# One load and six tiles for K, Q and V, and an issue order that expects loads later

## The chip, the cores and the metric

The kernel runs on one core of a Trainium2 chip. Its engines are TensorE (PE in the profile: matrix products, with PEld for its weight loads), VectorE (DVE), ScalarE (ACT), GpSimd (POOL) and SyncE (SP), which here only issues DMAs. Each engine takes its instructions in the order in which they stand in its program and waits on semaphores for the others. The metric is the device time of one execution in microseconds (us), the median over runs.

## The reference

Eight sequences of 576 tokens with eight heads of 64 go through causal attention with a window of 128 positions and a linear bias by distance. The result, 4,608 tokens of 512 numbers, goes through an MLP with a ratio of polynomials as activation:

```python
scores = scale * q @ k.T                       # per batch and head
mask = (rel >= 0) & (rel < 128)
scores = where(mask, scores - slope[h] * abs(rel), -1e9)
attn = softmax(scores)                         # sum + 1e-9 in the denominator
x = (attn @ v)                                 # to 4608 x 512
h = x @ w_in                                   # 512 -> 2048
g = (a0 + a1*h + a2*h**2 + a3*h**3) / (1 + |b0|*|h| + |b1|*h**2 + 1e-6)
out = g @ w_out                                # 2048 -> 512
```

The weights w_in and w_out come in 64-bit floats, which the kernel reads as pairs of 32-bit words.

## The kernel before, in words

Tokens lie in 36 blocks of 128. The MLP works on 17 tiles of them: the first and the last of three blocks, the others of two (`MLP`). Attention works on units: two heads (one of four pairs) and one or two blocks (`TILES`). The first tile has eight units: four of its first block, which use the tiles kq_first and v_first, and four of the other two blocks. Every other unit loads its keys and queries into a tile kq and its values into a tile v, four tiles of each in turn (lines 372 to 378).

A unit goes like this: TensorE makes the scores (sc, line 432); VectorE adds the bias and finds the row's extreme (line 458); ScalarE takes the exponential (line 463); VectorE takes sums and reciprocals (st, lines 471 and 472); POOL scales the probabilities (pr, line 473); TensorE transposes them (pt, line 484); ScalarE copies them out (p_all, line 488); POOL masks both copies (line 492); TensorE multiplies with the values (px, line 517); ScalarE and VectorE write x (lines 525 and 527).

The weights are cut in 16 chunks. Loads raw_w0 to raw_w31 bring them: an even number 2c is the w_in half of chunk c, the odd one 2c + 1 its w_out half (the name has the number only up to 15). Each is converted from 64 to 32 bits: POOL scales the upper words (line 578), ScalarE converts the lower (cv, line 579), VectorE joins them (lines 580 and 581, w32 or w in the trace). From load 16 on, w_in loads share one buffer and w_out loads another, so that each is issued when the one before it has been converted.

In the first tile's MLP (plain fp32) each chunk has an up-projection (h, lines 621 and 627), the activation, which ends with VectorE's g (line 657), and a down-projection for three blocks into three accumulators (acc, line 677). On the way POOL makes the gating terms (g_q, lines 645 and 647). The tiles h stand in three PSUM slots, one of which holds the third accumulator during the first tile. After that the weights are split into a high and a low part (lines 595 and 596, w_spare and w_lo, on POOL or VectorE), and all other tiles use three products of the parts.

The order of all this is set by a planner (`Plan.order`). Every operation has a due time, engines on which it may run with a cost on each, and what it depends on. The planner walks through time and gives each engine the ready operation that is due first. Due times come from some 35 numbers (A0, JL, C0, S0 and so on). The emitted program then keeps each engine's order; the chip sets the times. SP issues all DMAs; the eight semaphores for them are used in turn.

## Time and profile before

| | us |
|---|---|
| median of 3 runs (1047.11 to 1050.35) | 1047.44 |
| profiled execution | 1048.82 |
| its span, first to last instruction | 1047.1 |
| PE busy (97%) | 1019.4 |
| DVE busy (75%) | 781.3 |
| ACT busy (64%) | 671.9 |
| POOL busy (49%) | 511.5 |

Busy time is the union of an engine's instructions. A busy TensorE is not TensorE at its peak, since matmuls overlap and their ends are modelled. The granted clock is the share of TensorE's full clock (2.4 GHz) that it was given; 0.5 is 1.2 GHz. Idle time before an instruction is put down to the engine or DMA whose semaphore came last.

### The profile page before, as it was taken

What the parts mean: (1) busy time and instruction counts of PE and PEld (TensorE: products, weight loads), DVE (VectorE), ACT (ScalarE), POOL (GpSimd) and SP (SyncE); (2) the same over time, 40 slices, a digit from 0 to 9 for tenths busy, and PEclk for the clock granted to TensorE, in tenths of its full rate; (3) what the DMA queues carried; (4) which work ended last, traced back from release to release, by engine and by line L of the source; (5) the groups of instructions that cost most, each with busy time, mean ns of one, the idle gap of its engine ahead of it and who ended that gap; (6) DMA issues with size and microseconds to landing.
All of it is one profiled execution on the core that took longest, in us unless ns stands there. A gap on an engine that the chain in (4) does not pass through costs nothing.

```text
span 1047.1 us, 21020 instructions
## 1 busy us (share of the span) xinstructions
PE 1019.4 (97%) x7687; PEld 852.1 (81%) x7687; DVE 781.3 (75%) x1921; ACT 671.9 (64%) x1574; POOL 511.5 (49%) x579
## 2 busy tenths in 40 slices
PE   6799989999999999999999999999999999999998
PEld 4554458888888888888888888888888888888997
DVE  4887878877777777777777777777777777776775
ACT  5665678666666666666666666666665666666664
POOL 2754498544444444444444444444444444454442
PEclk7899999999999999999999999999999999999999
DMA  8815421111111121111110211111121112110000
GB/s 291 294 36 183 148 73 41 47 42 44 64 47 61 47 72 46 62 44 64 46 56 28 66 46 57 56 41 62 46 67 39 46 44 63 43 65 2 21 1 30
DMA packets 45271, 68.86 MB, mean 66 GB/s; under 512 B 4464, under 2 KB 29936, under 8 KB 45168
## 3 DMA queue, kind: packets, MB, share of 16 engines
q1 hardware_dynamic: 45168, 67.52, 19.6%
q8 instruction: 60, 0.98, 0.4%
q14 instruction: 43, 0.35, 0.1%
HBM read 58.07 MB, written 9.44 MB: 64 GB/s over the span
## 4 chain that ended last, share of the span: by engine, by line
PE 89%; DMA 3%; ACT 2%; DVE 2%; POOL 2%; issue 1%; SPq 0%; DVEq 0%; ACTq 0%; POOLq 0%
PE h L621 38%; PE acc L677 36%; PE px L517 7%; PE sc L432 5%; PE pt L484 3%; DMA raw_w<-in_w_in 2%; DMA raw_w<-in_w_out 1%; POOL w_lo L596 1%; ACT cv L579 1%; ACT pr L463 0%; DMA id_sb<-in_ident 0%; POOL g_q L647 0%; PE h L627 0%; DVE w L581 0%; POOL pr L473 0%
## 5 line engine op out<-in xcount | busy, mean ns | idle before, releaser
L621 PE MATMUL h<-x_hi,wi_hi 128*128 128x256 f32 (+1 forms) x1024 | 305.4, 298 | 2.5 <-ACT o L705 1.9
L621 PE MATMUL h<-x_lo,wi_hi 128*128 128x256 f32 (+1 forms) x1024 | 291.4, 285 | 0.0
L645 POOL TENSOR_SCALAR g_q<-g_u,babs 128x512 f32<-128x512 f32 (+1 forms) x152 | 115.2, 758 | 336.0 <-ACT g_u L644 328.7
L621 PE MATMUL h<-x_hi,w_lo 128*128 128x256 f32 (+1 forms) x960 | 272.8, 284 | 0.0
L621 PEld LDWEIGHTS h<-x_lo,wi_hi 128*128 128x128 f32 x1024 | 192.9, 188 | 38.9 <-issue 1.4
L621 PEld LDWEIGHTS h<-x_hi,wi_hi 128*128 128x128 f32 x1024 | 192.8, 188 | 36.6 <-issue 12.6
L677 PE MATMUL acc<-wo_hi,g_h 128*128 128x512 f32 x528 | 207.9, 394 | 0.0
L677 PE MATMUL acc<-wo_hi,g_l 128*128 128x512 f32 x528 | 200.5, 396 | 0.0
L677 PE MATMUL acc<-w_lo,g_h 128*128 128x512 f32 x495 | 194.5, 393 | 0.0
L647 POOL TENSOR_TENSOR g_q<-g_q,g_u 128x512 f32<-128x512 f32 (+1 forms) x152 | 189.3, 1245 | 9.5
L653 DVE SCALAR_TENSOR_TENSOR g_q<-g_q,h 128x512 f32<-128x512 f32 (+1 forms) x152 | 100.2, 659 | 122.6 <-ACT h L652 119.8
L621 PEld LDWEIGHTS h<-x_hi,w_lo 128*128 128x128 f32 x960 | 182.0, 190 | 0.0
L644 ACT ACTIVATE g_u<-h 128x512 f32<-128x512 f32 (+1 forms) x152 | 87.8, 577 | 111.9 <-PE h L621 110.9
L650 ACT ACTIVATE g_u<-g_q,guard 128x512 f32<-128x512 f32 (+1 forms) x152 | 106.5, 701 | 82.4 <-POOL g_q L647 79.5
L648 DVE TENSOR_TENSOR g_p<-h,g_p 128x512 f32<-128x512 f32 (+1 forms) x152 | 100.6, 662 | 69.0 <-ACT g_p L646 68.1
L473 POOL TENSOR_TENSOR pr<-pr,st 128x512 f32<-128x512 f32 (+1 forms) x76 | 76.2, 1003 | 89.5 <-DVE st L472 49.2
L463 ACT ACTIVATE pr<-pr,st 128x128 f32<-128x128 f32 x288 | 112.4, 398 | 8.5 <-DVE st L458 8.1
L646 ACT ACTIVATE g_p<-h,na 128x512 f32<-128x512 f32 (+1 forms) x152 | 114.9, 756 | 0.0
L492 POOL TENSOR_SCALAR_AFFINE_SELECT p_all<-p_all 128x512 f32<-128x512 f32 (+1 forms) x144 | 90.3, 627 | 50.3 <-ACT p_all L488 47.6
L661 ACT CAST g_h<-h 128x512 fp32r<-128x512 f32 (+1 forms) x136 | 78.7, 579 | 53.2 <-DVE h L660 53.0
L649 DVE SCALAR_TENSOR_TENSOR g_p<-g_p,na,h 128x512 f32<-128x512 f32 (+1 forms) x152 | 108.7, 715 | 2.7
L654 DVE SCALAR_TENSOR_TENSOR h<-g_p,na,h 128x512 f32<-128x512 f32 (+1 forms) x152 | 109.5, 721 | 0.0
(69 smaller groups left out, 1601.0 us busy)
## 6 DMA issues: line engine op xcount, KB each, us to landing
kq<-in_kqv SPq DMA_DIRECT2D x68, 320.0 KB, 3.3
v<-in_kqv SPq DMA_DIRECT2D x68, 192.0 KB, 2.6
out<-o SPq DMA_DIRECT2D x33, 256.0 KB, 2.0
raw_w<-in_w_in SPq DMA_DIRECT2D x16, 512.0 KB, 4.5
raw_w<-in_w_out SPq DMA_DIRECT2D x16, 512.0 KB, 5.8
bias_t<-in_bias SPq DMA_DIRECT2D x44, 64.0 KB, 2.3
kq<-in_kqv SPq DMA_DIRECT2D x4, 192.0 KB, 2.4
out<-o SPq DMA_DIRECT2D x6, 128.0 KB, 1.8
```

The costliest lines, as they stand in the source:

```text
L463: nc.scalar.activation(ap(pr)[:, y, :], ap(pr)[:, y, :], AF.Exp, bias=ap(st)[:, y : y + 1], scale=-1.0, accum_out=ap(st)[:, 4 + y : 5 + y])
L492: plan.op(A + D2 + 0.6 - 0.1 * k, cost, lambda e, k=k, sign=sign: nc.gpsimd.affine_select(out=side(k), in_=side(0), pattern=[[0, 2], [0, m ...
L621: nc.tensor.matmul(h(n), w[:, k, :], x[:, k, :], start=(k == 0 and m == 0), stop=(k == NKC - 1 and m == len(seq) - 1))
L645: plan.op(E, {"g": tsc}, lambda e: nc.gpsimd.tensor_scalar(v(g_q), v(g_u), ap(babs)[:, 1:2], ap(babs)[:, 0:1], ALU.mult, ALU.add), reads=[ ...
L646: plan.op(E, {"a": act(W, 1, 2) - 20}, lambda e: nc.scalar.activation(v(g_p), v(h_s), AF.Identity, bias=ap(na)[:, 2:3], scale=ap(na)[:, 3: ...
L647: plan.op(E, {"g": ttc}, lambda e: nc.gpsimd.tensor_tensor(v(g_q), v(g_q), v(g_u), ALU.mult), reads=[(g_q, 0), (g_u, 0)], writes=[(g_q, 0)])
L648: plan.op(E, {"v": dve(W)}, lambda e: nc.vector.tensor_tensor(v(g_p), v(h_s), v(g_p), ALU.mult), reads=[(h_s, 0), (g_p, 0)], writes=[(g_p, ...
L649: plan.op(E, {"v": dve(W, 1)}, lambda e: stt(v(g_p), v(g_p), ap(na)[:, 1:2], v(h_s), ALU.add, ALU.mult), reads=[(h_s, 0), (g_p, 0)], write ...
L650: plan.op(E, {"a": act(W, 0, 1)}, lambda e: nc.scalar.activation(v(g_u), v(g_q), AF.Ln, bias=guard, scale=1.0), reads=[(g_q, 0)], writes=[ ...
L653: plan.op(E, {"v": dve(W)}, lambda e: stt(v(g_q), v(g_q), GUARD, v(h_s), ALU.add, ALU.mult), reads=[(g_q, 0), (h_s, 0)], writes=[(g_q, 0)])
L654: plan.op(E, {"v": dve(W, 1)}, lambda e: stt(v(h_s), v(g_p), ap(na)[:, 0:1], v(h_s), ALU.add, ALU.mult), reads=[(g_p, 0), (h_s, 0)], write ...
L677: nc.tensor.matmul(ap(accs[t][i]), x[:, sl], w, start=(c == 0 and part == 0 and m == 0), stop=(c == NFC - 1 and (part == 1 or t == 0) and ...
```

## The change

For every unit but those of the first block, K, Q and V come in one load of 512 KB into one tile of 1,024 columns, and there are six such tiles. For the first block the keys and queries come in two loads in place of four, and the values in one. In the planner a load's user is taken to start 1,500 ns after the load's end (30 before), and SP is taken to be busy while eight loads are under way. Most of the numbers for due times have new values.

```diff
+LANES = 8
...
+        ("s", "p"): 1500, ("s", "v"): 1500, ("s", "a"): 1500, ("s", "g"): 1500,
...
                     if e == "s":
-                        free_at[e] = t + 475
                         dma_free = max(dma_free, t + 475 + 650) + cost
                         o.end = dma_free + 1000
+                        landed.append(o.end)
+                        free_at[e] = max(t + 475, landed[-LANES] if len(landed) >= LANES else 0.0)
...
-    sb4 = ctx.enter_context(tc.tile_pool(name="sb4", bufs=4))
+    sbk = ctx.enter_context(tc.tile_pool(name="sbk", bufs=6))
...
-    C0, DC, CO, DO, WL = 2.025, 6.35, 24.27, 5.33, 4.229
-    S0, DS, SL, AW, BL = 120.399, 2.316, 3.017, 27.807, 7.326
+    C0, DC, CO, DO, WL = -2.492, 6.391, 23.755, 5.295, 4.229
+    S0, DS, SL, AW, BL = 113.646, 2.291, 2.644, 27.807, 7.466
...
-            plan.op(u0 - JL, {"s": 364}, lambda e: eng[e].dma_start(ap(first_kq)[:, p], src[:, P : 3 * P]), writes=[(first_kq, p)])
-            plan.op(u0 - JL + VL, {"s": 182}, lambda e: eng[e].dma_start(ap(first_v)[:, p], src[:, 4 * P :]), writes=[(first_v, p)])
+            if p == 0:
+                firsts = kqv[o : o + NPAIR * P * W].rearrange("(p q w) -> q p w", p=NPAIR, q=P)
+                for g in ((0, 1), (1, NPAIR)):
+                    plan.op(u0 - JL, {"s": 364 * (g[1] - g[0])}, lambda e, g=g: eng[e].dma_start(ap(first_kq)[:, g[0] : g[1]], firsts[:, g[0] : g[1], P : 3 * P]), writes=[(first_kq, y) for y in range(*g)])
+                plan.op(u0 - JL + VL, {"s": 728}, lambda e: eng[e].dma_start(ap(first_v), firsts[:, :, 4 * P :]), writes=[(first_v, y) for y in range(NPAIR)])
...
-        kq = slot(sb4, [P, KMAX + QMAX], F32, "kq")
-        v = slot(sb4, [P, KMAX], F32, "v")
-        after = 1000 * (u0 - AW) if t else 0.0
-        plan.op(u0 - JL, {"s": 2002 * (W - ks) / 1408}, lambda e: eng[e].dma_start(ap(kq)[:, : W - ks], src[:, : W - ks]), writes=[(kq, 0)], after=after)
-        plan.op(u0 - JL + VL, {"s": 2002 * ks / 1408}, lambda e: eng[e].dma_start(ap(v)[:, :ks], src[:, W - ks :]), writes=[(v, 0)], after=after)
+        kqv_sb = slot(sbk, [P, WMAX], F32, "kqv")
+        plan.op(u0 - JL, {"s": 2002 * W / 1408}, lambda e: eng[e].dma_start(ap(kqv_sb)[:, :W], src), writes=[(kqv_sb, 0)], after=1000 * (u0 - AW) if t else 0.0)
```

The order of the instructions moves on all engines. Three places are shown; in a row stand the line, the instruction, and the tiles with the numbers that tell buffers apart, written tile first. Lines of the new kernel have numbers higher by three here. A DMA's shape is in elements: four bytes each, two for the bias.

The first place is the start of the program on SP and on POOL. SP before:

```order
L368 DMA kq_first_84<-in_kqv 128x256 x3
L314 DMA bias_first_91<-in_bias 128x1024
L368 DMA kq_first_84<-in_kqv 128x256
L369 DMA v_first_96<-in_kqv 128x128
L377 DMA kq_99<-in_kqv 128x640
L369 DMA v_first_96<-in_kqv 128x128
L311 DMA id_sb_115<-in_ident 128x256
L369 DMA v_first_96<-in_kqv 128x128
L377 DMA kq_125<-in_kqv 128x640
L369 DMA v_first_96<-in_kqv 128x128
L378 DMA v_137<-in_kqv 128x384
L573 DMA raw_w0_143<-in_w_in 128x4x256
```

and now:

```order
L317 DMA bias_first_84<-in_bias 128x1024
L374 DMA kq_first_87<-in_kqv 128x256
L374 DMA kq_first_87<-in_kqv 128x3x256
L314 DMA id_sb_92<-in_ident 128x256
L576 DMA raw_w0_95<-in_w_in 128x4x256
L375 DMA v_first_98<-in_kqv 128x4x128
L381 DMA kqv_101<-in_kqv 128x1024
```

POOL before, from its first work on (pr are probabilities, units 1 to 5 in this order):

```order
L473 TENSOR_TENSOR pr_120<-pr_120,st_121 128x256
L473 TENSOR_TENSOR pr_128<-pr_128,st_129 128x256
L578 TENSOR_SCALAR raw_w0_143<-raw_w0_143 128x512
L473 TENSOR_TENSOR pr_170<-pr_170,st_171 128x256
L473 TENSOR_TENSOR pr_205<-pr_205,st_206 128x256
L578 TENSOR_SCALAR raw_w2_201<-raw_w2_201 128x512
L578 TENSOR_SCALAR raw_w4_213<-raw_w4_213 128x512
L473 TENSOR_TENSOR pr_266<-pr_266,st_267 128x512
```

and now:

```order
L581 TENSOR_SCALAR raw_w0_95<-raw_w0_95 128x512
L476 TENSOR_TENSOR pr_125<-pr_125,st_126 128x256
L476 TENSOR_TENSOR pr_144<-pr_144,st_145 128x256
L581 TENSOR_SCALAR raw_w2_110<-raw_w2_110 128x512
L476 TENSOR_TENSOR pr_188<-pr_188,st_189 128x256
L476 TENSOR_TENSOR pr_214<-pr_214,st_215 128x256
L581 TENSOR_SCALAR raw_w4_154<-raw_w4_154 128x512
L581 TENSOR_SCALAR raw_w6_161<-raw_w6_161 128x512
L476 TENSOR_TENSOR pr_258<-pr_258,st_259 128x512
```

The first weight load moves from the fourteenth place on SP to the fifth; on POOL the scaling of each early weight load moves ahead by about two instructions.

The second place is POOL in the first tile's MLP, at the gating (g_q, two instructions a chunk) of chunks 6 and 7. Before, with the loads 20 (raw_w_838), 22 (raw_w_892) and 19 (raw_w_898):

```order
L645 TENSOR_SCALAR g_q_868<-g_u_855,babs_229 128x384
L578 TENSOR_SCALAR raw_w_838<-raw_w_838 128x512
L647 TENSOR_TENSOR g_q_868<-g_q_868,g_u_855 128x384
L578 TENSOR_SCALAR raw_w_892<-raw_w_892 128x512
L578 TENSOR_SCALAR raw_w_898<-raw_w_898 128x512
L645 TENSOR_SCALAR g_q_943<-g_u_931,babs_229 128x384
L647 TENSOR_TENSOR g_q_943<-g_q_943,g_u_931 128x384
```

and now, with the loads 20 (raw_w_816), 19 (raw_w_839) and 22 (raw_w_873):

```order
L581 TENSOR_SCALAR raw_w_816<-raw_w_816 128x512
L648 TENSOR_SCALAR g_q_858<-g_u_848,babs_169 128x384
L650 TENSOR_TENSOR g_q_858<-g_q_858,g_u_848 128x384
L581 TENSOR_SCALAR raw_w_839<-raw_w_839 128x512
L648 TENSOR_SCALAR g_q_892<-g_u_884,babs_169 128x384
L650 TENSOR_TENSOR g_q_892<-g_q_892,g_u_884 128x384
L581 TENSOR_SCALAR raw_w_873<-raw_w_873 128x512
```

Load 22 moves from ahead of the gating of chunk 7 to behind it. In the same way loads 24, 28 and 30 stand one or two chunks later against the gating.

The third place is POOL at the hand-over to the second tile, from the second gating instruction of the first tile's last chunk or shortly before it to the gating of the second tile's first pair of chunks. Before:

```order
L596 TENSOR_TENSOR w_spare_1298<-w32_0_249,wi_hi_1140 128x512
L645 TENSOR_SCALAR g_q_1326<-g_u_1296,babs_229 128x384
L596 TENSOR_TENSOR w_lo1_1331<-w32_1_363,wi_hi_1140 128x512
L647 TENSOR_TENSOR g_q_1326<-g_q_1326,g_u_1296 128x384
L596 TENSOR_TENSOR w_lo2_1354<-w32_2_332,wi_hi_1140 128x512
L596 TENSOR_TENSOR w_lo2_1354<-w32_2_332,wo_hi_1162 128x512
L596 TENSOR_TENSOR w_lo3_1382<-w32_3_447,wi_hi_1140 128x512
L596 TENSOR_TENSOR w_lo4_1401<-w32_4_530,wi_hi_1140 128x512
L645 TENSOR_SCALAR g_q_1415<-g_u_1405,babs_229 128x512
L473 TENSOR_TENSOR pr_1359<-pr_1359,st_1360 128x512
L647 TENSOR_TENSOR g_q_1415<-g_q_1415,g_u_1405 128x512
```

and now:

```order
L648 TENSOR_SCALAR g_q_1318<-g_u_1312,babs_169 128x384
L599 TENSOR_TENSOR w_spare_1321<-w32_0_164,wo_hi_1046 128x512
L650 TENSOR_TENSOR g_q_1318<-g_q_1318,g_u_1312 128x384
L476 TENSOR_TENSOR pr_1287<-pr_1287,st_1288 128x512
L599 TENSOR_TENSOR w_lo2_1364<-w32_2_321,wo_hi_1046 128x512
L599 TENSOR_TENSOR w_lo3_1383<-w32_3_341,wi_hi_1039 128x512
L495 AFFINE_SELECT p_all_1376<-p_all_1376 128x4x128
L648 TENSOR_SCALAR g_q_1396<-g_u_1386,babs_169 128x512
L495 AFFINE_SELECT p_all_1376<-p_all_1376 128x4x128
L650 TENSOR_TENSOR g_q_1396<-g_q_1396,g_u_1386 128x512
```

Three splittings leave POOL between the two gatings and the probabilities move ahead of the rest; on VectorE five splittings stand before the last g of the first tile, where three stood. On TensorE, the third pair of the second tile's up-projections, which waited for ScalarE's eviction of the third accumulator, stands behind four down-projections of the second tile, and its slot is one that VectorE frees.

## Rows read from the trace of the kernel before

**Rows 1.** Busy time by stretch. Columns: stretch in us from the span's start and its length, then busy us (and instructions) of PE, PEld, DVE, ACT and POOL, the granted clock, the busy share of the DMA engines, and GB/s.

```profile
0.00:10.00 10.00, 6.93 (x42) 2.94 (x43) 1.73 (x17) 3.30 (x10) 1.43 (x6) 0.95 0.73 201
10.00:20.00 10.00, 7.45 (x78) 4.54 (x77) 4.80 (x26) 5.78 (x24) 2.49 (x4) 0.54 0.95 323
20.00:30.00 10.00, 6.18 (x70) 5.30 (x74) 7.38 (x29) 5.86 (x19) 6.54 (x10) 0.83 0.93 326
...
40.00:43.00 3.00, 2.43 (x15) 1.72 (x16) 2.93 (x5) 1.83 (x3) 2.16 (x3) 0.50 0.93 247
43.00:47.00 4.00, 4.00 (x13) 3.21 (x12) 3.90 (x7) 2.85 (x5) 2.50 (x4) 0.56 1.01 371
...
80.00:100.00 20.00, 18.99 (x84) 9.57 (x82) 16.21 (x39) 12.09 (x28) 9.14 (x12) 1.00 0.42 143
...
155.00:160.00 5.00, 4.92 (x48) 4.25 (x48) 4.92 (x7) 2.71 (x6) 4.82 (x6) 0.66 0.14 52
...
170.00:1000.00 830.00, 830.00 (x6631) 725.96 (x6631) 620.86 (x1524) 538.63 (x1256) 398.23 (x440) 1.00 0.15 49
```

**Rows 2.** Waits of TensorE, longest in total first: engine, tile and line, what it waited for, us in total, times, longest. The first three are of 0 to 43 us, the fourth of 57 to 140 us, the last four of 140 to 170 us.

```profile
PE pt L484 <- POOL pr L473: 7.9, 5, 2.5
PE px L517 <- POOL p_all L492: 4.2, 3, 2.7
PE pt L484 <- DMA id_sb<-in_ident: 2.2, 1, 2.2
...
PE h L621 <- DVE g L657: 4.3, 7, 1.2
...
PE h L621 <- ACT o L705: 1.9, 1, 1.9
PE pt L484 <- POOL pr L473: 1.1, 1, 1.1
PE h L621 <- DVE g L657: 0.4, 1, 0.4
PE h L621 <- DVE g_l L662: 0.3, 1, 0.3
```

**Rows 3.** POOL in order of time, from the start: start in us, duration in us, line, operation, tiles, shapes, and in brackets the idle time before it and what ended it.

```profile
13.59 0.65 POOL L578 TENSOR_SCALAR raw_w<-raw_w 128x512 f32<-128x512 f32 x1 [3.88 <-DMA raw_w<-in_w_in]
...
21.30 1.03 POOL L473 TENSOR_TENSOR pr<-pr,st 128x512 f32<-128x512 f32 x1
23.38 0.65 POOL L578 TENSOR_SCALAR raw_w<-raw_w 128x512 f32<-128x512 f32 x1 [1.06 <-DMA raw_w<-in_w_in]
25.51 0.65 POOL L578 TENSOR_SCALAR raw_w<-raw_w 128x512 f32<-128x512 f32 x1 [1.47 <-DMA raw_w<-in_w_out]
...
39.87 0.64 POOL L492 TENSOR_SCALAR_AFFINE_SELECT p_all<-p_all 128x512 f32<-128x512 f32 x1
```

**Rows 4.** DMA issues by line: tiles, engine, count, KB each, median us from issue to landing.

```profile
kq<-in_kqv SPq DMA_DIRECT2D x68, 320.0 KB, 3.3
v<-in_kqv SPq DMA_DIRECT2D x68, 192.0 KB, 2.6
...
raw_w<-in_w_in SPq DMA_DIRECT2D x16, 512.0 KB, 4.5
raw_w<-in_w_out SPq DMA_DIRECT2D x16, 512.0 KB, 5.8
```

**Rows 5.** TensorE in order of time: the first up-projection of the first tile that needs all of its x.

```profile
43.39 3.42 PE L627 MATMUL h<-x_hi,w 128*128 128x256 f32 x8
```

**Rows 6.** VectorE in order of time, 104 to 107 us.

```profile
104.55 0.69 DVE L580 SCALAR_TENSOR_TENSOR cv<-raw_w,cv 128x512 int32<-128x512 int32 x1 [1.97 <-ACT cv L579]
...
106.94 0.55 DVE L657 SCALAR_TENSOR_TENSOR g<-g_q,h 128x384 f32<-128x384 f32 x1
```

**Rows 7.** TensorE in order of time, the same moment.

```profile
107.55 0.91 PE L621 MATMUL h<-x_hi,w 128*128 128x384 f32 x2 [1.20 <-DVE g L657]
```

**Rows 8.** Groups of instructions by line and shape: tiles, shapes, count, busy us, mean ns of one, idle us of the engine before them and what ended most of it. The first two are VectorE's in 57 to 147 us, the third is POOL's in 57 to 170 us.

```profile
L580 DVE SCALAR_TENSOR_TENSOR cv<-raw_w,cv 128x512 int32<-128x512 int32 x19 | 12.9, 694 | 7.0 <-ACT cv L579 3.3 <-POOL raw_w L578 2.9 <-POOL g_q L647 0.7
...
L596 DVE TENSOR_TENSOR w_lo<-w,wo_hi 128x512 fp32r<-128x512 f32 x3 | 3.0, 992 | 0.2 <-POOL w_lo L596 0.2
...
L578 POOL TENSOR_SCALAR raw_w<-raw_w 128x512 f32<-128x512 f32 x16 | 10.6, 661 | 21.9 <-DMA raw_w<-in_w_in 11.7 <-DMA raw_w<-in_w_out 9.5 <-DVE st L458 0.6
```

**Rows 9.** POOL in order of time at the gating of chunks 6 and 7.

```profile
80.72 1.01 POOL L647 TENSOR_TENSOR g_q<-g_q,g_u 128x384 f32<-128x384 f32 x1
87.17 0.66 POOL L578 TENSOR_SCALAR raw_w<-raw_w 128x512 f32<-128x512 f32 x1 [5.45 <-DMA raw_w<-in_w_in]
...
89.10 0.67 POOL L645 TENSOR_SCALAR g_q<-g_u,babs 128x384 f32<-128x384 f32 x1
```

**Rows 10.** POOL in order of time at the hand-over.

```profile
144.62 3.65 POOL L596 TENSOR_TENSOR w_lo<-w,wi_hi 128x512 fp32r<-128x512 f32 x2
148.25 1.30 POOL L645 TENSOR_SCALAR g_q<-g_u,babs 128x512 f32<-128x512 f32 x1
149.52 1.57 POOL L473 TENSOR_TENSOR pr<-pr,st 128x512 f32<-128x512 f32 x1
151.05 1.74 POOL L647 TENSOR_TENSOR g_q<-g_q,g_u 128x512 f32<-128x512 f32 x1
```

**Rows 11.** The w_in loads of line 573 issued from 60 to 120 us: time from issue to landing.

```profile
DMA to landing us min/median/max: 3.7/3.9/4.2
```

More of the change, by code (lines that the diff above doesn't have):

```diff
@@ L112, in order @@
         rings, free_at = {}, {**dict.fromkeys("pavg", 0.0), "s": 650.0}
-        dma_free, busy = 0.0, {}
+        dma_free, busy, landed = 0.0, {}, []
         for o in self.ops:
@@ L260, in banded_attention_ratio_mlp @@
     ps3 = ctx.enter_context(tc.tile_pool(name="ps3", bufs=3, space=PSUM))
-    count = {id(const): 1, id(ps1): 1, id(sb2): 2, id(sb3): 3, id(sb4): 4, id(ps3): 3}
+    count = {id(const): 1, id(ps1): 1, id(sb2): 2, id(sb3): 3, id(sbk): 6, id(ps3): 3}
     eng = {"p": nc.tensor, "a": nc.scalar, "v": nc.vector, "g": nc.gpsimd, "s": nc.sync}
@@ L265, in banded_attention_ratio_mlp @@
     SESSION = 290
-    A0, DA, T0, L0, L1 = -4.886, 1.542, 22.263, 90.555, 24.911
-    AOFF, D2, D3, JL, VL = -0.627, 1.814, 7.045, 8.441, 4.671
+    A0, DA, T0, L0, L1 = -0.833, 1.536, 22.263, 90.555, 24.812
+    AOFF, D2, D3, JL, VL = -0.627, 1.941, 7.045, 7.707, 4.001
     SP, SV, SA, SG = 0.204, 0.103, 0.021, 0.16
-    LL = 6.867
-    ML, ZA, ME, OE = 23.116, 0.956, -1.043, 9.542
-    C0, DC, CO, DO, WL = 2.025, 6.35, 24.27, 5.33, 4.229
-    S0, DS, SL, AW, BL = 120.399, 2.316, 3.017, 27.807, 7.326
+    LL = 13.858
+    ML, ZA, ME, OE = 23.116, 0.956, -1.043, 9.531
+    C0, DC, CO, DO, WL = -2.492, 6.391, 23.755, 5.295, 4.229
+    S0, DS, SL, AW, BL = 113.646, 2.291, 2.644, 27.807, 7.466
     plan = Plan({"p": 1000 * SP, "v": 1000 * SV, "a": 1000 * SA, "g": 1000 * SG})
@@ L373, in job @@
             return kt, qt, vt, [(first_kq, p)], [(first_v, p)]
-        kq = slot(sb4, [P, KMAX + QMAX], F32, "kq")
-        v = slot(sb4, [P, KMAX], F32, "v")
-        after = 1000 * (u0 - AW) if t else 0.0
-        plan.op(u0 - JL, {"s": 2002 * (W - ks) / 1408}, lambda e: eng[e].dma_start(ap(kq)[:, : W - ks], src[:, : W - ks]), writes=[(kq, 0)], after=after)
-        plan.op(u0 - JL + VL, {"s": 2002 * ks / 1408}, lambda e: eng[e].dma_start(ap(v)[:, :ks], src[:, W - ks :]), writes=[(v, 0)], after=after)
-        kt = lambda c0, c1: ap(kq)[:, c0:c1]
-        qt = lambda i: ap(kq)[:, ks + i * P : ks + (i + 1) * P]
-        vt = lambda b: ap(v)[:, b * P : (b + 1) * P]
-        return kt, qt, vt, [(kq, 0)], [(v, 0)]
+        kqv_sb = slot(sbk, [P, WMAX], F32, "kqv")
+        plan.op(u0 - JL, {"s": 2002 * W / 1408}, lambda e: eng[e].dma_start(ap(kqv_sb)[:, :W], src), writes=[(kqv_sb, 0)], after=1000 * (u0 - AW) if t else 0.0)
+        kt = lambda c0, c1: ap(kqv_sb)[:, c0:c1]
+        qt = lambda i: ap(kqv_sb)[:, ks + i * P : ks + (i + 1) * P]
+        vt = lambda b: ap(kqv_sb)[:, W - ks + b * P : W - ks + (b + 1) * P]
+        return kt, qt, vt, [(kqv_sb, 0)], [(kqv_sb, 0)]
     xs = {}
```

## The prediction

> **What bounds the kernel now.** I read the table of busy time by stretch first. From 170 to 1000 us TensorE is busy 830.00 of 830.00 us at a granted clock of 1.00 [rows 1]; the reader should see that nothing can be won there by waiting less, since no wait of TensorE is left. What the change can move lies before 170 us. I then read TensorE's waits in the stretches before that. They fall into three stages [rows 2]. In the start (0 to 43 us: attention of the first three blocks, in which only TensorE's waits of 7.9 us for POOL's scaling of the probabilities, 4.2 us for its masks and 2.2 us for the identity count) the engines wait for data. In the MLP of the first tile (57 to 140 us) TensorE waits 4.3 us in all, seven times, each time for VectorE's last step g. In the hand-over to the second tile (140 to 170 us) it waits 1.9, 1.1, 0.4 and 0.3 us. The third view is POOL's timeline: in the start POOL stands in front of weight loads, 13.59, 23.38 and 25.51 us being the ends of such waits [rows 3]; since it works in order, the scaling of the probabilities (pr) stands behind them.
>
> The profiled execution took 1048.82 us (span 1047.1 us and 1.7 us around it); the median of the three timed runs is 1047.44 us. I sum changes in us against the profiled execution and take the sum off the median.
>
> **Steady state, 170 us to the end: 0.** TensorE's instructions are the same in number and shape; only their order differs here and there. Every load of K, Q and V that used to be two is now one, and SP issues 77 fewer DMAs. No TensorE wait in this stretch names a load, so fewer or earlier ones hide nothing that is now seen: what covers the loads is TensorE's own work, and six tiles in place of four only widen the cover. If the cover went, a unit's scores would wait for a 512 KB load; the nearest rows are 3.3 us for the 320 KB part and 4.5 to 5.8 us for the 512 KB weights from issue to landing, once [rows 4]. I keep 0, with 0.5 us either way.
>
> **Step 1, the start: +1.7 us.** The order moves the first weight load from the fourteenth place on SP's queue to the fifth, and POOL's rows move with it: its first instruction is now the scaling of weight load 0, ahead of the first probabilities; and before the probabilities of the fifth unit it now scales loads 4 and 6, where before it scaled loads 2 and 4. Count the KB on the queue, each load by its size (the large ones in [rows 4]; the small ones are 64 to 256 KB by their shapes in the order). Up to and with weight load 0 there were 2,496 KB, now 1,408; up to load 6 there were 5,571 KB, now 6,083; up to the last load that POOL scales before the last mask of the first tile, 10,563 (load 7) and now 11,779 (load 9). Load 0 was scaled at 13.59 us; by bytes alone it now lands at 1,408 / 2,496 x 13.59 = 7.7 us. From 20 to 30 us the queue moved 326 GB/s, 318 KB a us [rows 1]. From 7.7 us at that rate, load 6 lands at 7.7 + 4,675 / 318 = 22.4 us, and by the bytes of before (5,571 KB at 23.38 us, 6,403 KB at 25.51 us [rows 3]) at 24.7 us. Add 0.65 us for its scaling: the fifth unit's probabilities start between 23.1 and 25.3 us, where they started at 21.30 us [rows 3]: +1.8 to +4.0 us. From there to the end of the last mask POOL has four scalings of probabilities at 1.04, eight masks at 0.64 and nine weight scalings at 0.66 us, 15.2 us; before it had one weight scaling less, 14.6 us, and took from 21.30 to 40.51 us for it, so 4.6 us were waits. With no wait it would now end at 23.1 + 15.2 = 38.3 us, 2.2 us sooner. With load 9 at 22.4 + 5,696 / 318 = 40.3 us, and its scaling and two masks behind it (1.9 us), it ends at 42.2 us, 1.7 us later. The bounds are thus -2.2 and +4.0 us; I take +1.7, the value of the row of 20 to 30 us, in which the same loads were under way. The first up-projection that needs all of x (43.39 us, eight matmuls in 3.42 us [rows 5]) moves with it. It ran at the lower level of TensorE's clock: granted 0.50 and 0.56 in 40 to 47 us, 1.2 GHz for most of it, after a stretch in which TensorE waited [rows 1, 2]. Its start stays as full of waits, so I leave that cost (4 us at 0.44 lost, 1.8 us) as it is; both ends are inside the bounds above.
>
> Before 10 us the queue moved 201 GB/s, and from 10 to 20 us 323 GB/s [rows 1]; four loads of 64 KB (v_first) and five of 128 KB are among the first thirteen. The Trainium skill (DMA: Bandwidth & Descriptors, Rules for kernel authors) says to merge many small transfers into one large one. By the rows nothing says whether size or the cold start makes the first 10 us slow, so the sum above takes the rate from later; by the rule the start would gain, which is the second rival.
>
> **Step 2, the MLP of the first tile: -3.8 us.** The path is seen once in full: VectorE waits 1.97 us for a converted weight load before 104.55 us, g ends at 107.49 us, and TensorE, which waited 1.20 us for it, starts at 107.55 us [rows 6, 7]. In this stretch VectorE waits 7.0 us before such conversions and POOL 21.2 us for loads (11.7 and 9.5 us) [rows 8]. The clearest wait of POOL is 5.45 us before 87.17 us, with the gating (g_q) of the next chunk queued behind the load [rows 9]. The new order puts that load's scaling behind the gating pair of chunk 7 instead of ahead of it, which is 0.67 + 1.01 us of work in front of it, and does the like for the w_in loads of chunks 12, 14 and 15. So when a load is late, what waits for it is the conversion of a later chunk, not the g that TensorE is about to read. VectorE's own work between two g's (0.55 to 0.7 us each, conversions 0.69) does not change in sum. I keep 0.5 us of the 4.3 us: the w_in load of chunk 13 is issued when a conversion is done that stands 1.2 us ahead of a g, VectorE wants it two conversions (1.4 us) after that g, and such a load takes 3.9 us to land [rows 11]. Bounds: -4.3 us (all of it) and +1.2 us (one more stall as long as the longest).
>
> **Step 3, the hand-over: -1.0 us.** Two stalls go. The third pair of the second tile took the PSUM slot of the third accumulator, whose eviction stood on ScalarE behind a logarithm that waited for POOL (1.9 us); now it takes a slot that VectorE frees, and four down-projections of the second tile stand before it. The transposes waited 1.1 us for probabilities behind six weight splittings and a gating on POOL [rows 2, 10]; now one splitting stands before them. That is -3.0 us. What is late next is the last g of the first tile: VectorE has five splittings before it where it had three, 0.99 us each [rows 8], +2.0 us, and the second pair waits for that slot. Bounds: -3.7 us (all four waits) and +3.0 us (five splittings delay and none of the stalls goes). The lower clock after these waits, 0.66 in 155 to 160 us [rows 1], costs 5 x 0.34 = 1.7 us and lies inside the bounds.
>
> **Sum.** 1.7 - 3.8 - 1.0 = -3.1 us: 1045.7 us for the profiled execution, 1044.3 us for the median.
>
> **Rivals.**
> 1. The stalls only move. VectorE is busy 16 of 20 us in the first MLP and has little room, so a delay of 1.7 us at the start could keep it behind TensorE all along. Then step 2 gives 1.7 us and steps 1 and 3 cancel it: 1047.4 us. For it: g of one chunk is followed by TensorE's use within 0.06 us [rows 6, 7]. Against: in the new order most g's stand several VectorE instructions earlier against TensorE's use.
> 2. The start gains as well: larger and fewer loads fill the queue from the first us, so that POOL never waits after the fifth unit and step 1 is its lower bound, -2.2 us. Sum -7.0 us: 1040.4 us. For it: 323 GB/s as soon as the queue is full. Against: 201 GB/s before.
> 3. Slower: POOL's wait for load 6 in front of the fifth unit's probabilities, at the upper bound of +4.0 us, and ScalarE's conversion of load 1 in front of that unit's copy of the transposes carry through the start, while step 2 gives only 0.8 us and step 3 nothing: +3.2 us, 1050.6 us. It decides if load 6 is scaled after about 25 us. For it: POOL did wait for each of these loads. Against: after 10 us the queue has no gap that six tiles would not close.
> That the change does not do what it says is no rival: the order of SP shows one load per unit.
>
> **How the numbers follow.** Forecast 0.42, rival 1 0.21, rival 2 0.24, rival 3 0.13. A difference of 0.3%, 3.1 us, is about what a measurement of this kernel can tell from no change. The forecast stands on that line, so half of it (0.21) counts as faster and half as the same: faster 0.45, same 0.42, slower 0.13. The range reaches from rival 2 to short of rival 3: 1040.0 to 1049.5 us.
>
> **What would show it.** Step 1: POOL's scaling of load 6 at 22 to 25 us, and the up-projection of eight matmuls at 42 to 47 us. Step 2: TensorE's waits for g in the first MLP under 1 us in sum, POOL's waits for loads well under 21 us. Step 3: no wait of TensorE for the eviction of an accumulator, a new one of 1 to 3 us for the last g. Wrong would be any TensorE wait after 170 us, or a start that ends before 41 or after 47 us.

## The result and the profile after

The new kernel took 1058.21 us (median of 4 runs, 1056.88 to 1059.37) where the kernel before took 1047.28 in the same session: the ratio is 1.0091, 95% interval 1.0078 to 1.0104, so it is slower by 0.9%. The profiled execution, the fastest of the four, took 1056.88 us, its span is 1055.2 us, and it is the one that the rows below are from; the other three had spans of 1056.3 to 1057.6 us at a mean granted clock of 0.983 to 0.985, where this one had 0.989.

Busy time by stretch, of the new kernel, columns as in [rows 1], with three stretches more:

```profile
0.00:10.00 10.00, 5.20 (x33) 2.28 (x33) 2.10 (x16) 3.78 (x10) 1.42 (x6) 1.00 0.75 240
10.00:20.00 10.00, 8.21 (x86) 5.08 (x86) 5.76 (x29) 5.97 (x25) 3.10 (x5) 0.52 1.04 392
20.00:30.00 10.00, 5.38 (x48) 3.96 (x50) 6.94 (x23) 5.11 (x16) 6.95 (x11) 0.84 1.05 395
40.00:43.00 3.00, 2.64 (x16) 1.73 (x18) 1.66 (x13) 2.75 (x11) 2.36 (x5) 0.50 0.63 183
43.00:47.00 4.00, 4.00 (x24) 3.13 (x21) 3.75 (x7) 2.89 (x6) 2.09 (x3) 0.80 0.86 275
50.00:60.00 10.00, 9.10 (x52) 5.64 (x51) 7.10 (x22) 4.83 (x16) 3.79 (x6) 0.83 0.05 15
60.00:80.00 20.00, 18.74 (x88) 10.17 (x87) 18.34 (x43) 14.22 (x33) 11.60 (x15) 1.00 0.23 75
...
170.00:1000.00 830.00, 827.88 (x6614) 721.05 (x6615) 622.14 (x1521) 533.42 (x1245) 396.12 (x437) 1.00 0.15 48
```

The same for the kernel before in the stretches that [rows 1] doesn't have:

```profile
50.00:60.00 10.00, 9.66 (x59) 5.46 (x59) 8.68 (x26) 7.64 (x21) 5.53 (x8) 1.00 0.11 40
60.00:80.00 20.00, 20.00 (x91) 10.86 (x90) 16.10 (x39) 11.84 (x29) 10.45 (x14) 1.00 0.24 72
```

From 170 us on TensorE lacks 2.12 us of 830, and its last wait of the hand-over ends at 175.4 us. So here too nearly all that matters comes before 190 us. The queue moved more per us than before in all of the first 30 us (240, 392 and 395 GB/s against 201, 323 and 326), yet from 50 to 60 us TensorE is behind: 9.10 us busy at a clock of 0.83.

TensorE's waits in the new kernel: the first line is of 57 to 140 us, the others of 140 to 190 us (columns as in [rows 2]):

```profile
PE h L624 <- DVE g L660: 4.2, 4, 1.9
...
PE acc L680 <- ACT g_h L664: 2.9, 2, 2.5
PE h L624 <- DVE g L660: 2.2, 1, 2.2
PE pt L487 <- POOL pr L476: 1.6, 1, 1.6
PE h L624 <- DVE g_l L665: 1.2, 1, 1.2
```

In the first MLP the wait for g is what it was, 4.2 us for 4.3. At the hand-over four waits of 3.7 us in sum have become waits of 7.9 us. Those for g_h and for pr stand at places where there was none; those for the last g and for g_l were 0.4 and 0.3 us before.

To see where time is lost when the order differs, I counted TensorE's work: each of its instructions at its length at full clock (0.84 ns a column in the first tile's MLP, the mean from 200 to 1000 us for the others), added up in the order of the trace. Time less that sum is what was lost by then, by waits and by the clock alike. The kernel before has lost 31.9 us at 60 us, 38.4 at 140, 44.4 at 190. Against it, the new kernel:

| lost more than before, us, by | 60 us | 140 us | 190 us | 980 us |
|---|---|---|---|---|
| new kernel | +3.5 | +3.1 | +7.7 | +8.6 |

That is +3.5 in the start, -0.4 in the first MLP, +4.6 at the hand-over and 0.9 later; the spans differ by 8.1 us. The count itself is good to about 1 us. For the start a single execution is less sure than that: three of the runs below have the new kernel's order up to 60 us, and counted in the same way they had lost 4.4, 5.2 and 5.6 us more than before by then. So the figures for the start are good to about 2 us.

### The profile page after: what moved, and what is told of

It is laid out like the page before. It is cut to its first block, busy times and chain, and to the rows that moved or that the text cites. A ratio compares the mean times of both kernels' runs of the same rounds, so it can differ in the third digit from the quotient of the medians.

```text
span 1055.2 us, 20925 instructions
## 1 busy us (share of the span) xinstructions
PE 1021.3 (97%) x7687; PEld 850.9 (81%) x7687; DVE 788.0 (75%) x1925; ACT 671.4 (64%) x1574; POOL 509.1 (48%) x575
## 4 chain that ended last, share of the span: by engine, by line
PE 88%; DVE 3%; DMA 3%; POOL 2%; ACT 2%; issue 1%; SPq 0%; ACTq 0%; POOLq 0%; DVEq 0%
PE h L624 38%; PE acc L680 36%; PE px L520 6%; PE sc L435 5%; PE pt L487 3%; POOL w_lo L599 1%; DMA raw_w<-in_w_out 1%; DMA kqv<-in_kqv 1%; DVE cv L583 1%; DVE w_lo L599 1%; ACT pr L466 0%; DMA kq_first<-in_kqv 0%; ACT cv L582 0%; DVE w L584 0%; DMA raw_w<-in_w_in 0%
```

## The experiments

**Which part of the change? Each alone, in the kernel before.**

The loads alone (the edit of lines 365 to 385 with six tiles; rules and numbers as before):

> The kernel before with only the loads changed: one load of 512 KB a unit, six tiles, the merged first loads; planner and numbers as before. Theory N (the new numbers cost the time, since they put VectorE's conversions and splittings in front of what TensorE waits for): within 2 us of before, 1045 to 1049 us. Theory L (the loads cost it: what they move on the queue is late): 1053 us or more. Theory R (the planner's two rules cost it): as N here.

The planner's rules alone:

> The kernel before with only the planner's two rules changed (users of a load start 1,500 ns after it, SP is busy while eight loads are under way). Theory R: 1053 us or more. Theories N and L: within 2 us of before, 1045 to 1049 us.

The numbers alone:

> The kernel before with only the numbers for due times changed; loads and planner as before. Theory N: as slow as the new kernel, 1055 to 1060 us, most of it lost before 60 us and from 150 to 185 us. Theories L and R: 1045 to 1049 us.

Measured: 1056.80, 1053.32 and 1059.72 us, beside 1048.22 for the kernel before (ratios 1.0080, 1.0039 and 1.0106, each interval within 0.003 of it). Each theory's own run came out in its range, and the other two theories, which held that part to be free (1045 to 1049 us), were wrong about it. So no one part is the cause: each alone costs 5 to 12 us, and all three together cost 11, less than the parts' sum of 25. What they have in common is that each gives another order.

So I tried the smallest cause of another order, one number of the kernel before:

```diff
-    C0, DC, CO, DO, WL = 2.025, 6.35, 24.27, 5.33, 4.229
+    C0, DC, CO, DO, WL = 2.025, 6.35, 24.47, 5.33, 4.229
```

> The kernel before, in which a single number is changed: the due times of the w_out loads come 0.2 us later (CO 24.27 to 24.47). Loads, tiles and rules are those of before. Theory T: 4 to 9 us slower, 1051 to 1056 us, lost between 40 and 190 us. Theories L and R (a part of the change costs the time): no change, 1046 to 1049 us.

Measured: 1055.99 us beside 1048.56 (1.0064, 1.0047 to 1.0080), as Theory T said: the medians are 7.4 us apart, with the loads, tiles and rules of before. Its waits of TensorE from 140 to 190 us:

```profile
PE pt L484 <- POOL pr L473: 3.9, 2, 2.8
PE h L621 <- DVE g L657: 2.6, 2, 1.6
PE px L517 <- POOL p_all L492: 1.0, 1, 1.0
PE h L621 <- DVE g_l L662: 0.8, 1, 0.8
```

8.3 us, for 3.7 before: the same kind of waits as in the new kernel, from a shift of the due times of 16 loads and their conversions by 0.2 us.

**Can the places be mended one by one?** The next runs keep the new kernel and move a few instructions behind or ahead of others, after the planner has set the order. First the three numbers of the splittings as before:

```diff
-    S0, DS, SL, AW, BL = 113.646, 2.291, 2.644, 27.807, 7.466
+    S0, DS, SL, AW, BL = 120.399, 2.316, 3.017, 27.807, 7.466
```

> The new kernel with the three numbers S0, DS and SL of before, which set when the weights are split at the hand-over; the order up to 130 us stays. If these three cause what is lost from 150 to 185 us (4.3 us more than before), the time falls by 3 to 5 us, to 1053 to 1055 us, and the waits of 2.5 us for g_h, 1.6 us for pr and 1.2 us for g_l go. If the hand-over is slow because VectorE comes into it late, it falls by less than 1 us and waits of the same sum stand there under other names.

Measured: 1056.51 us (1.0064, 1.0044 to 1.0085), 1.7 us under the new kernel (in another session) and short of the 3 to 5 us expected. The waits for the last g, for pr and for g_l are gone; in their place stand, from 140 to 190 us,

```profile
PE acc L681 <- ACT g_h L665: 3.8, 1, 3.8
PE px L521 <- POOL p_all L496: 1.4, 1, 1.4
```

5.2 us for 7.9. After the wait of 3.8 us the clock fell, as this stretch of the same run shows:

```profile
160.00:170.00 10.00, 6.56 (x29) 5.98 (x30) 8.83 (x14) 6.86 (x13) 8.81 (x7) 0.66 0.39 132
```

2.2 us of full speed went there (6.56 busy x 0.34), most of the 2.7 us that the waits gave back. Then the conversion of load 11 behind the first chunks:

```diff
+    ahead(op["a", 11], op["a", 16])
+    ahead(op["cv", 11], op["cv", 16])
+    ahead(op["w", 11], op["cv", 16])
```

> The new kernel, in which the conversion of weight load 11 (one instruction on ScalarE, two on VectorE, 1.4 us) stands behind the first two chunks' activation, as before, and not ahead of the first. Theory Q (TensorE's time goes where VectorE or POOL have other work queued in front of the activation): VectorE's first g_p comes 1.3 us earlier, TensorE's waits of 1.1 and 0.9 us for conversions at 50 us fall by about 1.3 us in sum, and the time by 1 to 3 us, to 1055 to 1057 us. Rival (the start is set by the landing of the loads and the clock): no change, 1057 to 1059 us.

Measured: 1057.21 us (1.0083, 1.0068 to 1.0098), in the rival's range and just outside Theory Q's. At 60 us the loss was 2.1 us smaller than in the new kernel, at 80 us about the same again. (Against the three runs with the new kernel's start it was 3.1 to 4.3 us smaller at 60 us and 0.9 to 2.3 at 80.) TensorE in this run, two moments (start, duration, idle time before):

```profile
50.54 0.94 PE L436 MATMUL sc<-kqv 64*64 64x128 f32 x24 [1.17 <-DVE w L585]
...
63.42 0.91 PE L625 MATMUL h<-x_hi,w 128*128 128x384 f32 x2 [2.77 <-DVE g L661]
```

VectorE just before the second moment:

```profile
60.90 0.69 DVE L584 SCALAR_TENSOR_TENSOR cv<-raw_w,cv 128x512 int32<-128x512 int32 x1
61.62 0.69 DVE L585 SCALAR_TENSOR_TENSOR w<-raw_w,cv 128x512 int32<-128x512 int32 x1
62.22 0.69 DVE L584 SCALAR_TENSOR_TENSOR cv<-raw_w,cv 128x512 int32<-128x512 int32 x1
62.82 0.55 DVE L661 SCALAR_TENSOR_TENSOR g<-g_q,h 128x384 f32<-128x384 f32 x1
```

Three steps of conversions now stand right in front of the second chunk's g where the new kernel had one, and the wait there grew from 1.26 to 2.77 us. The gain was real, and most of it was given back by 80 us. That VectorE has hardly any room there (18.34 of 20 us in 60 to 80) may be why, but it is not shown: the best kernel below has VectorE busy for 17.53 us of the same 20, and there TensorE is busy for all 20.

At the hand-over, splittings behind what TensorE waits for (the edit names nine, of which 14 to 16 keep their place on their engine, so that six move):

```diff
+    op["lo", 6].engine = "v"
+    behind(op["lo", 7], op["g", 0, 15])
+    behind(op["lo", 6], op["g", 0, 15])
+    behind(op["lo", 13], op["g", 1, 0])
+    for k in (14, 15, 16):
+        behind(op["lo", k], op["lo", k - 1])
+    behind(op["lo", 20], op["pr", 14])
+    behind(op["lo", 22], op["g", 1, 2])
+    behind(op["lo", 25], op["gl", 1, 2])
```

> The new kernel, in which at the hand-over eight splittings stand behind an activation step or the probabilities instead of ahead of them (one of them goes from POOL to VectorE); the number of splittings is the same. Theory Q: the waits of 2.2 us for the last g, 2.5 us for g_h, 1.6 us for pr and 1.2 us for g_l fall from 7.6 to under 4 us in sum and the time by 3 to 5 us, to 1053 to 1055 us. Rival (VectorE and POOL have too much work between 145 and 175 us in any order): the sum of the waits stays over 6 us and the time within 1 us of the new kernel.

Measured: 1058.87 us (1.0099, 1.0084 to 1.0115), no gain. TensorE's waits from 140 to 190 us, the three largest:

```profile
PE acc L681 <- ACT g_h L665: 2.9, 2, 1.9
PE h L625 <- DVE g L661: 1.5, 1, 1.5
PE h L625 <- DVE g_l L666: 1.3, 2, 0.7
...
```

7.3 us in all; the big ones are smaller and others have come to them. That is the rival's outcome, though its reason (too much work in any order) will not stand.

In the first MLP, and all three edits together:

> The new kernel, in which at three places of the first tile's MLP a conversion or the next chunk's g_p steps stand behind g instead of ahead of it, and ScalarE's logarithm and exponential of chunk 8 ahead of the next chunk's absolute value. Theory Q: the three waits for g (1.3, 1.9 and 0.9 us) fall to under 1.5 us in sum and the time by 2 to 3 us, to 1055 to 1056 us. Rival (g is late because the weights are): the waits and the time stay.

> All three edits together. Theory Q: the gains add to 6 to 10 us, 1048 to 1052 us, about the kernel before. If the time that one edit frees is lost at the next stage, 1054 us or more.

Measured: 1060.78 and 1058.56 us, both above Theory Q's ranges. These two say little: the edit put the g_p steps of chunk 9 behind the exponential that overwrites what they read, so that chunk's activation is not the reference's, and g_p waits for that exponential, a wait that I had not meant to add.

Is it the count of splittings on VectorE? In the new kernel VectorE has 17 of the 32 and POOL 15, before it was 13 and 19.

```diff
+    for k in (8, 14, 18, 20):
+        op["lo", k].engine = "v"
```

> The kernel before, in which four of the 32 splittings go from POOL to VectorE, 17 in place of 13, as in the new kernel and in each of the slower ones. Theory V (the hand-over is slow because VectorE has four splittings more, 0.7 to 1.8 us each): the waits of TensorE from 140 to 190 us grow by 2 to 5 us and the time to 1049 to 1052 us. Rival (VectorE has room there, 6.94 us busy of 10 in 150 to 160 us): within 1 us of before.

Measured: 1047.50 us (0.9989, 0.9979 to 0.9999). Theory V falls; the count costs nothing where the order leaves room.

**What does a fitted order make of the same parts?** The due-time numbers were searched anew, with the planner alone, until the end by its own clock was earliest; nothing else was changed. First the merged loads with the old rules:

> The merged loads and the six tiles with the planner's rules of before and due-time numbers that were searched for anew, until the planner's own clock was shortest. Theory T (neither loads nor rules cost time; each change gives an order that nobody has fitted, and an order that is not fitted loses 5 to 12 us before 190 us): 1047 us or less, 10 us under the same loads with the old numbers (1056.8 us). Theory L (the loads cost it): 1053 us or more, since the loads are the same as there.

The new kernel's loads and both rules:

> The new kernel with loads, tiles and the two rules, and numbers searched for anew in the same way. Theory T: 1047 us or less. Theory M (the rules make the planner expect loads 3 us and more later than they land, 38.15 us for weight load 14 that landed at 36.6 us and 40.1 for load 3 that had landed at 27 us, so an order that fits the planner's clock doesn't fit the chip): slower than the retuned loads without the rules by 3 us or more, 1048 to 1056 us.

(The 40.1 us given there for load 3 is the planner's time for its use, not for its landing.) Measured: 1043.13 us (0.9941, 0.9926 to 0.9956) and 1054.09 us (1.0046, 1.0031 to 1.0061). The first has the loads, tiles and rules of the first experiment (1056.80 us) and differs from it in numbers alone: 13.7 us lie between them (ratios to before of 0.9941 and 1.0080), and in 140 to 190 us TensorE has not one wait. So the loads don't cost the time. The second came out as theory M said. So each rule by itself, the old loads as a control, and second sets of numbers:

> The merged loads and six tiles, of the two rules only the one by which SP is busy while eight loads are under way, numbers searched anew. If the 1,500 ns before a load's users is what makes the order unfit: 1042 to 1047 us. If this rule is: 1050 us or more. If only both together do: 1042 to 1047 us here and in the next run.

> The same with the other rule only, a load's users start 1,500 ns after it. If these 1,500 ns make the order unfit: 1050 us or more. If the rule on eight loads does: 1042 to 1047 us.

> Loads, tiles and rules of before, numbers searched anew in the same way and for as long as for the merged loads. Theory T (the loads are neutral, an order's fit is all): within 2.5 us of the merged loads searched anew (1043.1 us), 1041 to 1046 us. If the loads and the six tiles are worth 5 us by themselves: 1047 us or more, no better than before.

> The new kernel's loads, tiles and both rules with a second set of numbers, from another search. Theory M (both rules together make the order unfit): 1050 us or more again. If the first set was a bad draw: 1042 to 1047 us, as with each rule alone.

> Loads, tiles and rules of before with a second set of numbers, from another search. If the merged loads are worth several us in a fitted order (the start of the first set lost 4 us more by 60 us than the three fitted orders with merged loads): 1046 us or more again. If the first set was a bad draw: 1041 to 1045 us.

> The merged loads with the rules of before and numbers chosen to bear loads and engines a few per cent off the planner's own figures. If fit to the chip is what counts: as fast as the first set (1043.1 us) or up to 2 us faster, 1040 to 1044 us. If the first set was luck: 1046 us or more.

| loads, rules | numbers | us | ratio to before, 95% | lost by 60 / 140 / 190 us, against before |
|---|---|---|---|---|
| merged, old rules | searched | 1043.13 | 0.9926 to 0.9956 | -0.8 / -3.6 / -9.0 |
| merged, old rules | chosen to bear a few per cent | 1045.74 | 0.9955 to 0.9978 | +0.4 / -2.3 / -5.7 |
| merged, rule of eight | searched | 1043.24 | 0.9939 to 0.9973 | -1.9 / -4.3 / -6.1 |
| merged, rule of 1,500 ns | searched | 1045.12 | 0.9954 to 0.9978 | -1.5 / -5.0 / -8.2 |
| merged, both (new kernel) | first set | 1054.09 | 1.0031 to 1.0061 | +2.1 / -1.2 / +0.6 |
| merged, both (new kernel) | second set | 1042.87 | 0.9925 to 0.9956 | -4.5 / -6.8 / -8.7 |
| old, old | first set | 1050.03 | 1.0002 to 1.0022 | +1.4 / -0.1 / -1.3 |
| old, old | second set | 1044.32 | 0.9931 to 0.9975 | -1.0 / -2.8 / -4.3 |

Neither rule alone makes the order unfit (1043.24 and 1045.12 us). The first set for the old loads missed Theory T's 1041 to 1046 us. The numbers chosen to bear a few per cent gave 1045.74 us, between the two ranges stated for them, so that run decides nothing. Theory M falls with the second set: the same loads, tiles and rules as the new kernel, with other numbers, take 1042.87 us where the kernel before took 1049.20 on the same chip. This version beats both kernels, the new one by 1.5% (1.0091 to 0.9941, in different sessions). What the merged loads are worth by themselves stays open: the second set for the old ones gave 1044.32 us, and the 1.5 us between the best of each are less than two sets of one kind differ by (2.6 to 11 us). Theory T is what remains, and its strict form is wrong too: an end that the planner puts early is no promise, since two of the seven sets that were searched for the earliest end gave 1050 us and more. In the first set for both rules the loss comes after 190 us (+0.6 there, +5.3 at 980 us). From there to 980 us TensorE waits 0.5 us in all and has the clock at 1.00, so neither explains it, and its cause stays open.

The second set is the best kernel here. Its numbers:

```diff
-    A0, DA, T0, L0, L1 = -0.833, 1.536, 22.263, 90.555, 24.812
-    AOFF, D2, D3, JL, VL = -0.627, 1.941, 7.045, 7.707, 4.001
-    SP, SV, SA, SG = 0.204, 0.103, 0.021, 0.16
-    LL = 13.858
-    ML, ZA, ME, OE = 23.116, 0.956, -1.043, 9.531
-    C0, DC, CO, DO, WL = -2.492, 6.391, 23.755, 5.295, 4.229
-    S0, DS, SL, AW, BL = 113.646, 2.291, 2.644, 27.807, 7.466
+    A0, DA, T0, L0, L1 = 1.3196, 1.16563, 22.263, 92.8172, 24.7258
+    AOFF, D2, D3, JL, VL = 0.154072, 2.50672, 8.18304, 13.328, 8.38041
+    SP, SV, SA, SG = 0.118028, 0.0899765, -0.0379476, 0.127445
+    LL = 6.96256
+    ML, ZA, ME, OE = 27.9823, 0.924374, -3.75721, 4.54333
+    C0, DC, CO, DO, WL = 4.56286, 6.51872, 26.6176, 4.97545, 5.18672
+    S0, DS, SL, AW, BL = 122.161, 2.26931, 7.42405, 25.906, 8.5593
```

Its stretches and its first up-projection of eight matmuls:

```profile
40.00:43.00 3.00, 3.00 (x13) 2.12 (x12) 2.93 (x6) 2.12 (x4) 1.20 (x2) 1.00 0.91 288
43.00:47.00 4.00, 4.00 (x32) 2.32 (x32) 3.72 (x7) 2.39 (x5) 2.98 (x5) 1.00 0.86 300
50.00:60.00 10.00, 10.00 (x28) 5.05 (x27) 9.71 (x29) 7.62 (x20) 6.37 (x9) 1.00 0.01 2
...
39.41 1.89 PE L630 MATMUL h<-x_hi,w 128*128 128x256 f32 x8
```

Its waits of TensorE, the largest of 57 to 140 us, and the two largest of 140 to 190 us:

```profile
PE h L624 <- DVE g L660: 2.1, 2, 1.2
...
PE acc L680 <- ACT g_h L664: 1.4, 1, 1.4
PE pt L487 <- POOL pr L476: 1.3, 2, 0.7
...
```

In all they are 2.3 us in the first MLP for 4.2 in the new kernel, and 3.2 us at the hand-over for 7.9. Too much work in any order is not the reason: the run of 1045.12 us (rule of 1,500 ns) has 17 splittings on VectorE and 15 on POOL, as the new kernel has, and by 190 us it had lost 8.2 us less than the kernel before. (The best kernel has 13 and 19.) From 40 to 47 us and from 50 to 60 us it has the clock at 1.00, where the new kernel had 0.50, 0.80 and 0.83.

## Why the prediction was wrong

It said 1044.3 us, by -3.1 us on the profiled execution; that execution came out at +8.1 us. What failed is the summing of single waits: each step took one wait away or put one in, and left out what the new order puts in front of TensorE's next instructions, on VectorE in step 1, on ScalarE in step 2 and behind the last g in step 3. By its steps:

**Steady state, 0.** About right: 0.9 us lost between 190 and 980 us, a little over the 0.5 us either way. The waits of 1.6, 0.4 and 1.2 us after 170 us, named as what would show it wrong, belong to the hand-over, which lasts longer than I had drawn it.

**Step 1, +1.7 us for the start; lost 3.5 us by 60 us.** POOL's last mask of the first tile ended at 42.2 us, as the sum said, and the up-projection of eight matmuls came at the time forecast. Both came by another way, and the loss went on after them:

```profile
21.59 0.65 POOL L581 TENSOR_SCALAR raw_w<-raw_w 128x512 f32<-128x512 f32 x1 [1.95 <-DMA raw_w<-in_w_in]
...
37.45 1.04 POOL L476 TENSOR_TENSOR pr<-pr,st 128x512 f32<-128x512 f32 x1 [3.26 <-DVE st L475]
...
40.28 0.64 POOL L581 TENSOR_SCALAR raw_w<-raw_w 128x512 f32<-128x512 f32 x1
40.88 1.34 POOL L495 TENSOR_SCALAR_AFFINE_SELECT p_all<-p_all 128x512 f32<-128x512 f32 x2
...
44.86 1.89 PE L630 MATMUL h<-x_hi,w 128*128 128x256 f32 x8
```

Load 6 was scaled at 21.59 us, earlier than my 22 to 25, since from 10 to 20 us the queue moved 392 GB/s, which is 383 KB a us, and not the 318 that I took from [rows 1]; the fifth unit's probabilities started 0.9 us later than before, not 1.8 to 4.0. The sum had POOL wait for load 9 before its last masks; that load was there (its scaling at 40.28 us has no wait), and POOL had stood 3.26 us behind VectorE instead. So the 42.2 us were met by luck, and the up-projection began 1.5 us later than before. The step that failed is the one that counted POOL's instructions up to the last mask and let the start end there. VectorE is what TensorE waits for next: it is full from 40 to 47 us in [rows 1] (2.93 of 3.00 and 3.90 of 4.00 us), which I had and did not use. In the new order it does 14 conversions of loads ahead of the first g_p where it did 13. A conversion works in a PSUM buffer that the scores use in turn (lines 410 and 567 before, 413 and 570 now), so TensorE stood behind it, in the new kernel:

```profile
49.79 0.43 PE L435 MATMUL sc<-kqv 64*64 64x128 f32 x2 [1.11 <-DVE w L584]
51.12 1.35 PE L435 MATMUL sc<-kqv 64*64 64x128 f32 x21 [0.90 <-DVE w L584]
```

and after these waits it had the clock at 0.83 from 50 to 60 us, 9.10 x 0.17 = 1.5 us. The forecast left the clock as it was.

**Step 2, -3.8 us for the first MLP; -0.4 us.** POOL's waits for loads fell as I had said, from 21.2 to 9.7 us, by this group of 57 to 170 us:

```profile
L581 POOL TENSOR_SCALAR raw_w<-raw_w 128x512 f32<-128x512 f32 x15 | 9.9, 666 | 9.7 <-DMA raw_w<-in_w_in 5.5 <-DMA raw_w<-in_w_out 4.2
```

and TensorE's wait for g did not follow. The sentence that failed is that a late load now delays "the conversion of a later chunk, not the g", with only 0.5 us kept: it took the loads for the only thing in front of g. In the longest of the new waits no load is late. POOL, ScalarE (two rows) and TensorE:

```profile
99.31 1.00 POOL L650 TENSOR_TENSOR g_q<-g_q,g_u 128x384 f32<-128x384 f32 x1
...
100.80 0.49 ACT L647 ACTIVATE g_u<-h 128x384 f32<-128x384 f32 x1 [2.04 <-PE h L624]
101.18 0.61 ACT L653 ACTIVATE g_u<-g_q,guard 128x384 f32<-128x384 f32 x1
...
105.57 0.91 PE L624 MATMUL h<-x_hi,w 128*128 128x384 f32 x2 [1.86 <-DVE g L660]
```

The gating of chunk 8 is ready at 100.31 us, but on ScalarE its logarithm (line 653) stands behind the absolute value of chunk 9, which waits for TensorE; behind it on VectorE a g_p of chunk 9 and a conversion come ahead of g. I had followed only POOL's queue and VectorE's; ScalarE's order was not in the sum.

**Step 3, -1.0 us for the hand-over; +4.6 us.** Right in its parts: the wait of 1.9 us for an eviction and that of 1.1 us for the first probabilities are gone, and the last g came with a wait of 2.2 us, of which I had said 1 to 3 (the term of +2.0). What failed is "what is late next is the last g", as though nothing came after it. The splittings that were moved off POOL's stretch before the first probabilities stand behind it, and the next three things that TensorE needs were late in turn. VectorE and TensorE ahead of the largest of them:

```profile
157.58 0.69 DVE L599 TENSOR_TENSOR w_lo<-w,wo_hi 128x512 fp32r<-128x512 f32 x1 [1.17 <-POOL w_lo L599]
158.19 0.68 DVE L656 SCALAR_TENSOR_TENSOR g_q<-g_q,h 128x512 f32<-128x512 f32 x1
...
161.47 0.50 PE L680 MATMUL acc<-wo_hi,g_h 128*128 128x512 f32 x1 [2.54 <-ACT g_h L664]
```

A splitting on VectorE waited 1.17 us for one on POOL, with the activation of the first pair queued behind it. The upper bound that I gave, +3.0 us, has no sum behind it, and in its words only the five splittings before the last g delay; the waits after that were in no term.

**The rivals.** The first (the stalls only move) is what the runs with moved instructions showed, but in the new kernel the moved stalls were longer. The second (larger loads let the start gain) is borne out for the queue and not in this order; with other numbers the same loads and rules lose 4.5 us less by 60 us than the kernel before. The third had the size nearest to the result, and not its mechanism: load 6 was not late. What none of them held is that a new order as such can lose: of six changes to the kernel before without new numbers fitted to them (three parts, all of them, one number, four splittings on another engine) five lost 5 to 12 us and one, the splittings, lost nothing. Why the numbers of this change fit so badly is not settled; that they are its cause is shown by the second set.

One number could have given the sign before any run, and the forecast didn't use it: the end that the planner itself works out for its order. Worked out from the kernels, it is 1046.4 us before and 1055.3 us for the new kernel, +8.9 where +10.9 was measured; for the loads, the rules, the numbers and the one number alone it is 1052.4, 1056.1, 1053.2 and 1053.5 us. Two of these five have other rules than the kernel before, the rules alone and the new kernel, so that their ends are not strictly comparable with its own. And among the searched sets it doesn't rank: both sets for the new kernel's rules end at 1043.4 to 1043.5 us by the planner, and they measured 1054.09 and 1042.87 us.

## What to carry to other kernels

Where every engine's order is fixed by a planner and VectorE or POOL are nearly full, the waits of single places don't add up to a forecast: most of what an edit gained at one place here was given back a few us later, and a change of order can lose until the numbers are fitted again, as five of six did here. Judge such a change (loads, tiles, rules) only after fitting both versions, with more than one set of numbers each, since here sets of one kind differed by 2.6 to 11 us. For a forecast, read the planner's own end first, which had the sign here but not the ranking of fitted sets. Then follow each queue that stands in front of what TensorE waits for, ScalarE's too, to the next thing that is late and the one after it.

## What the runs showed of the hardware

Loads of 512 KB with rows of 4 KB instead of parts of 320 and 192 KB raised the queue's rate from 323 and 326 to 392 and 395 GB/s between 10 and 30 us, with the DMA engines' busy share at 1.04 and 1.05 for 0.95 and 0.93. From 10 to 20 us the seven kernels here with the old loads moved 322 to 346 GB/s, and the thirteen with the merged ones 363 to 406. The Trainium skill (DMA: Bandwidth & Descriptors, Rules for kernel authors) says to merge many small transfers into one large one; the trace agrees, by a fifth.

A splitting takes 0.69 us on VectorE and 1.28 us on POOL by itself. When both split at once one takes longer by about the other's time: here VectorE (first row) and POOL (second) start together, POOL ends at 174.12 us and VectorE 0.55 us later.

```profile
172.84 1.83 DVE L599 TENSOR_TENSOR w_lo<-w,wo_hi 128x512 fp32r<-128x512 f32 x1
...
172.83 1.29 POOL L599 TENSOR_TENSOR w_lo<-w,wi_hi 128x512 fp32r<-128x512 f32 x1
```

The Trainium skill (SBUF — State Buffer, SBUF: two separate sides) says that an operation of GpSimd that reads SBUF and one of VectorE with two inputs in SBUF share a pair of ports as an exclusive lock, for a whole instruction; the trace agrees, by the 1.83 us. VectorE's groups from 135 to 200 us in the new kernel show what it sums to:

```profile
L599 DVE TENSOR_TENSOR w_lo<-w,wo_hi 128x512 fp32r<-128x512 f32 x9 | 9.7, 1074 | 2.4 <-POOL w_lo L599 2.4
L599 DVE TENSOR_TENSOR w_lo<-w,wi_hi 128x512 fp32r<-128x512 f32 x7 | 7.8, 1121 | 1.7 <-POOL w_lo L599 1.3 <-POOL w_spare L599 0.3
```

16 splittings take 17.5 us where 16 x 0.69 = 11.0 would do. The prediction had them at 0.99 us each [rows 8], and only for the two that were new before the last g.

The same eight matmuls of the first up-projection took 3.42 us before [rows 5], at a granted clock of 0.55 in just that stretch (1.2 GHz, the lower of its two levels, for most of it), and 1.89 us in the new kernel and in the best one, at 1.00 in theirs (2.4 GHz). 3.42 x 0.55 is 1.88 us, so the clock is the whole difference.
